# Moving the V-tile loads of a decode attention kernel from SyncE's DMA queue to ScalarE's

## The chip, the cores and the metric

One core of a Trainium2 chip runs the whole program once. The metric is device time in microseconds of that launch: 406.5 us, the median of three runs (406.42 to 406.69). The core has a matrix engine (TensorE, PE in the profile), a vector engine (VectorE, DVE), an activation engine (ScalarE, ACT), GpSimd (POOL) and SyncE (SP). Each runs its own list of instructions in order and waits on semaphores that the others and the DMA transfers raise. Sixteen DMA engines move data between the chip's main memory and the on-chip buffers.

## The reference, cut to what matters

One token (S = 1, D = 1024) passes an attention block with a cache of 65536 keys in 4 groups, each shared by 8 of 32 query heads of width 128, and, beside it, a small MLP mixer; both are added to the input.

```python
xn = _layernorm(x)
q  = xn @ wq                                   # 32 heads x 128
scores = einsum(q, k) * 128 ** -0.5            # k, v: 4 groups x 65536 keys x 128, bf16
p  = softmax(scores)
A  = einsum(p, v).reshape(4096) @ wo
h  = gelu(layernorm(xn) @ w1)                  # its parts are shifted by one or two tokens
x1 = xn + shifted(h) @ w2
B  = x1 + gelu(layernorm(x1) @ w3) @ w4
return x + A + B
```

With one token, the shifted parts of `h` are all zero; the kernel keeps those products. The two caches are 67 MB each, and with the weights nearly 170 MB are read once.

## The kernel before, in words

Everything large arrives in one of five equal buffers, the slots (`SLOTS = 5`, pool `big`, L61), each 128 partitions x 32 KB, 4 MiB in all. `items` (L82 to L91) lists the loads in order: two halves of wq; then for each of 4 groups g and 4 blocks r of 16384 keys the pair K(g,r), V(g,r); two halves of w3 after block (0,1), w1 after (1,1), a quarter of wo after each group; at the end w2 and w4 in five pieces of 16, 8, 2, 1 and 1 rows per partition. In this text K12 is group 1, block 2. wo, w1 and w2 loads are 2 MiB, the w3 halves 3.5 MiB.

The loop at L440 asks for the loads up to four items ahead (`ensure`, L129), then records the work on the current one. A load can only be issued when its slot is open, that is, when the last reader of the slot's former tenant is done. All loads of `items` are issued by SyncE (L118), so they stand in one queue in this order.

Work on a K tile (`compute_K`, L342): four in-place 32x32 transposes on VectorE (L353), each followed by eight scoring products of 512 keys on TensorE (L357). After the last of these the slot is open. Then comes a short chain: `mx` on VectorE (L361), a TensorE transpose (L363), `m8` and `rep` on VectorE (L365, L367), a TensorE transpose back (L370), `nball` (L372), the exponential on ScalarE (`p_sb`, L374), and its transpose on VectorE (`pT`, L377).

Work on a V tile (`compute_V`, L382): 32 products with `pT` on TensorE (L389), after which the slot is open, and a copy `ob` on ScalarE (L394). After the fourth block `group_end` (L399) merges the four blocks: `negmg`, `wts`, `og` (L402 to L409), `pm_e` (L417, L419), `msk`, `rl`, `o5`, `oT5` (L421 to L428). `compute_wo` (L431) multiplies `oT5` with the wo quarter into the output rows (`psB`, L160); w2 and w4 are added to the same rows at the end.

The order on each engine is not that of the source. The framework's scheduler takes the recorded instructions and orders each engine's list by when it expects operands to be there, and it also decides which open slot the next tile gets. In the built kernel of before, VectorE does the whole chain of one K tile up to `pT` before it starts transposes of the next one. Two small loads of the input go over ScalarE's queue at the start (L123, L125), and four small transfers of the MLP over GpSimd's queue (L288, L290).

Of the kernel before, what the change touches and what calls it, by code (L numbers as in the profile page):

```python
# [22 lines left out]
def kernel(  # L23
# [14 lines left out]
    nc = tc.nc  # L38
# [56 lines left out]
    def slot():  # L95
        return big.tile([P, KEYS], BF16, name="slot")

    def issue(item):
        kind = item[0]
        t = slot()  # L100
        if kind == "wq":
            src = wq_v[:, 4 * item[1]:4 * item[1] + 4, :].rearrange("p c n -> p (c n)")
        elif kind == "w3":
            src = w3_v[:, 4 * item[1]:4 * item[1] + 4, :].rearrange("p c n -> p (c n)")
        elif kind == "w4":
            c0 = w4_start[item[1]]
            src = w4_v[:, c0:c0 + W4_PIECES[item[1]], :].rearrange("p c n -> p (c n)")
        elif kind == "w1":
            src = w1_v
        elif kind == "w2":  # L110
            src = w2_v
        elif kind == "wo":
            src = wo_v[item[1]]
        else:
            cache = A_k_cache if kind == "K" else A_v_cache
            _, g, r = item
            src = cache[0, g, r * KEYS:(r + 1) * KEYS, :].rearrange("(p k) d -> p (k d)", p=P)
        nc.sync.dma_start(out=t[:, 0:src.shape[-1]], in_=src)  # L118
        st[item] = t


# [7 lines left out]
    def ensure(upto):  # L129
        while n_issued[0] <= min(upto, len(items) - 1):  # L130
            issue(items[n_issued[0]])
            n_issued[0] += 1
# [85 lines left out]
    for cg in range(4):  # L218
        nc.vector.tensor_copy(out=selbig[:, cg, :].rearrange("p (hl dd) -> p hl dd", dd=16),
                              in_=sel32[:, 8 * cg:8 * cg + 8].unsqueeze(2).to_broadcast([P, 8, 16]))  # L220
    sel8big = const.tile([P, P], F32, name="sel8big")
    nc.vector.tensor_copy(out=sel8big[:].rearrange("p (hl dd) -> p hl dd", dd=16),
                          in_=sel8[:].unsqueeze(2).to_broadcast([P, 8, 16]))
# [3 lines left out]
    for b in range(2):  # L227
        for par in range(2):
            nc.vector.tensor_copy(out=psel[:, 2 * b + par, :].rearrange("p (a i) -> p a i", a=4),  # L229
                                  in_=iv[:, b, par, :].unsqueeze(1).to_broadcast([P, 4, 32]))  # L230
# [242 lines left out]
```

## Time and profile before

| what | us |
|---|---|
| median of three runs | 406.5 (406.42 to 406.69) |
| the profiled execution's own time | 406.69 |
| its span | 404.8 |
| PE / DVE / ACT busy | 245.7 / 215.7 / 37.7 |
| share of the span that the 16 DMA engines spend on SyncE's queue (q1) | 98.0% |
| mean rate of the DMA engines | 420 GB/s |
| issue to landing of a K load, of a V load (median) | 34.5, 35.5 |

The page of the profile gives the busy time of each engine, then the span in 40 slices (a digit is a busy share in tenths), the DMA queues, the chain of work that ended last, and groups of equal instructions with their busy time, the mean of one in ns, and the idle time in front of them with what ended most of it. In the waits, a row reads: engine and line, what it waited for, us in total, times, longest. In the timeline a row reads: start, us, engine, line, operation; SPq and ACTq rows are the issuing of a DMA, and the idle time before them is found in the waits of the queue. The instruction's source line is given as L353.

### The profile page before, as it was taken

How to read it: one execution, taken by the hardware profiler on the slowest of the kernel's cores; microseconds unless marked ns; L12 is line 12 of the kernel's file. 1: busy time of each engine (PE TensorE's matmuls, PEld its weight loads, DVE VectorE, ACT ScalarE, POOL GpSimd, SP SyncE). 2: the span in 40 equal slices, each digit the busy share in tenths (PEclk: the TensorE clock that was granted, in tenths of full speed). 3: DMA queues.
4: the chain of work that ended last, by engine and by line, in shares of the span. 5: the costliest groups of instructions: out<-in, count | busy, mean ns of one | idle time of the engine just before them, and what ended most of it. 6: DMA issues, size and time to landing. Idle time of an engine off the chain costs nothing.

```text
span 404.8 us, 3326 instructions
## 1 busy us (share of the span) xinstructions
PE 245.7 (61%) x1400; PEld 95.7 (24%) x1400; DVE 215.7 (53%) x235; ACT 37.7 (9%) x60; POOL 11.2 (3%) x30
## 2 busy tenths in 40 slices
PE   0385565328475847557657948384659474758456
PEld 0132222103132312112223313131233121213122
DVE  0419474017484848346665847475748383838500
ACT  0101101100201010120210010101010101010100
POOL 5001000000000000000010000000000000000000
PEclk9998878857795778768595868888958797679898
DMA  8999999999999999999999999999999999999993
GB/s 363 415 424 449 418 426 434 430 418 444 434 408 439 447 416 419 458 418 416 447 431 413 437 444 414 435 440 418 430 440 424 428 439 427 425 437 413 440 415 134
DMA packets 7065, 170.11 MB, mean 420 GB/s; under 512 B 1023, under 2 KB 1033, under 8 KB 1418
## 3 DMA queue, kind: packets, MB, share of 16 engines
q1 hardware_dynamic: 6772, 169.87, 98.0%
q8 instruction: 11, 0.18, 0.2%
q0 software_dynamic: 128, 0.02, 0.0%
q10 hardware_dynamic: 150, 0.01, 0.0%
q14 instruction: 4, 0.03, 0.0%
HBM read 169.88 MB, written 0.01 MB: 420 GB/s over the span
## 4 chain that ended last, share of the span: by engine, by line
DMA 54%; PE 23%; DVE 17%; ACT 2%; another core or an unknown queue 1%; issue 1%; DVEq 0%; ACTq 0%
DMA slot<-in_A_k_cache_dram 44%; DVE slot L353 11%; PE sc L357 10%; DMA slot<-in_B_w_dram 7%; PE psB L160 5%; PE oacc L389 4%; DMA x_bf<-in_A_x_dram 3%; DVE pT L377 2%; DVE mx L361 2%; ACT p_sb L374 2%; PE rows L244 1%; PE pm_e L417 1%; DVE m L365 0%; PE pm_mx L363 0%
## 5 line engine op out<-in xcount | busy, mean ns | idle before, releaser
L353 DVE STREAM_TRANSPOSE slot<-slot 128x2048 f32<-128x2048 f32 x64 | 142.3, 2281 | 61.1 <-DMA slot<-in_A_k_cache_dram 61.1
L357 PE MATMUL sc<-slot,qst 128*128 128x512 bf16 x512 | 131.6, 411 | 40.9 <-DVE slot L353 40.9
L389 PE MATMUL oacc<-slot,pT 128*32 128x512 bf16 x512 | 56.0, 616 | 48.0 <-DVE pT L377 48.0
L357 PEld LDWEIGHTS <-qst 128*128 128x128 bf16 x512 | 51.6, 103 | 125.1 <-issue 45.9
L361 DVE TENSOR_REDUCE mx<-sc 128x1 f32<-128x1024 f32 x16 | 19.6, 1225 | 34.7 <-PE sc L357 34.7
L374 ACT ACTIVATE p_sb<-sc,nball 128x1024 bf16<-128x1024 f32 x16 | 17.8, 1114 | 209.8 <-DVE nball L372 209.8
L389 PEld LDWEIGHTS <-pT 128*32 128x32 bf16 x512 | 17.5, 139 | 75.0 <-DVE pT L377 49.4
L377 DVE STREAM_TRANSPOSE pT<-p_sb 128x1024 bf16<-128x1024 bf16 x16 | 19.9, 1245 | 23.3 <-ACT p_sb L374 23.3
L244 PE MATMUL rows<-slot,xpad 128*32 128x512 bf16 (+1 forms) x144 | 13.6, 509 | 6.1 <-DMA slot<-in_B_w_dram 6.1
L363 PE MATMUL pm_mx<-ident_f,mx 128*1 128x128 f32 x16 | 4.3, 270 | 21.1 <-DVE mx L361 21.1
L160 PE MATMUL psB<-slot,oT 128*1 128x512 bf16 x64 | 12.6, 564 | 4.3 <-DVE oT L428 4.3
L394 ACT COPY ob<-oacc 128x512 f32<-128x512 f32 x12 | 7.0, 586 | 58.6 <-PE oacc L389 58.6
L160 PE MATMUL psB<-slot,dst_h 128*1 128x512 bf16 x56 | 7.9, 444 | 3.2 <-DMA slot<-in_B_w_dram 3.2
L370 PE MATMUL pm_mx<-ident_f,rep 1*128 1x1 f32 x16 | 3.5, 222 | 9.9 <-DVE rep L367 9.9
L417 PE MATMUL pm_e<-og,selbig 128*128 128x128 f32 x32 | 7.4, 403 | 3.4 <-DVE og L409 3.4
L244 PEld LDWEIGHTS <-xpad 128*32 128x32 bf16 x144 | 5.7, 127 | 15.0 <-issue 13.7
L172 PE MATMUL pm_ln<-ln_rowsum_a,ones_f 128*128 128x1 f32 x2 | 0.6, 348 | 13.6 <-DVE psel L229 13.6
L337 DVE CAST out<-psB 64x256 bf16<-64x256 f32 x1 | 0.4, 417 | 15.2 <-ACT out L336 15.2
L363 PEld LDWEIGHTS pm_mx<-ident_f,mx 128*1 128x1 f32 x16 | 1.3, 79 | 29.0 <-DVE mx L361 29.0
L417 PEld LDWEIGHTS pm_e<-og,selbig 128*128 128x128 f32 x32 | 6.3, 293 | 6.7 <-DVE og L409 6.7
L365 DVE TENSOR_REDUCE m<-pm_mx 1x8 f32<-1x128 f32 x16 | 4.4, 278 | 5.8 <-PE pm_mx L363 5.8
L374 ACT ACT_TABLE_LOAD x3 | 3.8, 1283 | 35.6 <-DVE nball L372 35.6
(97 smaller groups left out, 79.3 us busy)
## 6 DMA issues: line engine op xcount, KB each, us to landing
slot<-in_A_k_cache_dram SPq DMA_DIRECT2D x16, 4096.0 KB, 34.5
slot<-in_A_v_cache_dram SPq DMA_DIRECT2D x16, 4096.0 KB, 35.5
slot<-in_A_wq_dram SPq DMA_DIRECT2D x2, 4096.0 KB, 21.4
slot<-in_A_wo_dram SPq DMA_DIRECT2D x4, 2048.0 KB, 38.4
slot<-in_B_w_dram SPq DMA_DIRECT2D x2, 3584.0 KB, 42.6
slot<-in_B_w_dram SPq DMA_DIRECT2D x3, 2048.0 KB, 26.9
slot<-in_B_w_dram SPq DMA_DIRECT2D x1, 4096.0 KB, 27.8
slot<-in_B_w_dram SPq DMA_DIRECT2D x1, 512.0 KB, 16.1
```

The lines of the kernel that those rows point to most:

```text
L160: nc.tensor.matmul(psB[32 * j:32 * j + 1, :], lhsT=lhsT, rhs=rhs, start=(not row_started[j]), stop=False, tile_position=(0, 32 * j), skip_ ...
L244: nc.tensor.matmul(acc[32 * j:32 * j + 32, bk, 0:width], lhsT=xp[:, c, :], rhs=wt[:, cl, ch * width:(ch + 1) * width], start=(c == 0), sto ...
L353: nc.vector.transpose(out=kf[:, cg, :], in_=kf[:, cg, :])
L357: nc.tensor.matmul(sc[:, hf, :], lhsT=qst[g % 2][:, o:o + 128], rhs=kr[:, cg, hf, :, bp // 2, :, bp % 2], start=(cg == 0 and bp == 0), sto ...
L361: nc.vector.reduce_max(out=mx[:], in_=sc[:].rearrange("p h n -> p (h n)"), axis=AX.X)
L363: nc.tensor.transpose(pm[0:1, 0:P], mx[:, 0:1], ident_f[:])
L365: nc.vector.reduce_max(out=m8[:], in_=pm[0:1, 0:P].rearrange("o (j h) -> o h j", h=8), axis=AX.X)
L374: nc.scalar.activation(out=p_sb[:], in_=sc[:], func=ACTF.Exp, bias=nball[:, r:r + 1], scale=SCALE, accum_out=lall[:, r:r + 1])
L377: nc.vector.transpose(out=pT[:], in_=p_sb[:])
L389: nc.tensor.matmul(oacc[32 * u:32 * (u + 1), :], lhsT=pT[:, hf, 32 * t:32 * (t + 1)], rhs=vt[:, :, hf, t, :], start=(hf == 0 and t < 4), s ...
L394: nc.scalar.copy(out=ob[:], in_=oacc[:])
L417: nc.tensor.matmul(pe[:, 0:P], lhsT=selbig[:, cg, :], rhs=og[:, 128 * cg:128 * (cg + 1)], start=(cg == 0), stop=(cg == 3))
```

## The change

Where `issue` used to call SyncE for every tile, it now calls ScalarE for V tiles and SyncE for all others. The list of loads, the number of slots and the lookahead stay.

```diff
             src = cache[0, g, r * KEYS:(r + 1) * KEYS, :].rearrange("(p k) d -> p (k d)", p=P)
-        nc.sync.dma_start(out=t[:, 0:src.shape[-1]], in_=src)
+        eng = nc.scalar if kind == "V" else nc.sync
+        eng.dma_start(out=t[:, 0:src.shape[-1]], in_=src)
         st[item] = t
```

In the changed kernel every line after L117 has a number that is one higher, since the edit adds a line.

## The prediction

> **What bounds the kernel now.** I read the page's head and slices, then the queues, the chain, the waits, and the timeline of SyncE's issues.
>
> ```profile
> span 404.8 us, 3326 instructions
> DMA  8999999999999999999999999999999999999993
> q1 hardware_dynamic: 6772, 169.87, 98.0%
> DMA 54%; PE 23%; DVE 17%; ACT 2%; another core or an unknown queue 1%; issue 1%; DVEq 0%; ACTq 0%
> L353 DVE STREAM_TRANSPOSE slot<-slot 128x2048 f32<-128x2048 f32 x64 | 142.3, 2281 | 61.1 <-DMA slot<-in_A_k_cache_dram 61.1
> ```
>
> The 16 DMA engines are busy from the second slice to the last, 98.0% of it by q1, SyncE's queue; the vector engine idles 61.1 us for K tiles. The bound is the stream: 169.87 MB that may never pause. K03 (group 0, block 3) is first touched at 109.37 after 45.09 MB, K32 at 344.51 after 145.75 MB: 100.66 MB in 235.14 us, 428 GB/s. A 4 MiB tile takes 9.80 us, and a tile lands at bytes/428 GB/s + 4.0 us, 3.3 of which are latency (the first issue is at 0.74).
>
> What keeps the stream from pausing is the list of loads issued ahead:
>
> ```profile
> 120.33 0.33 SPq L118 DMA_DIRECT2D slot<-in_A_k_cache_dram  x1
> 129.20 0.33 SPq L118 DMA_DIRECT2D slot<-in_A_v_cache_dram  x1
> 136.98 0.33 SPq L118 DMA_DIRECT2D slot<-in_B_w_dram  x1
> 144.62 0.33 SPq L118 DMA_DIRECT2D slot<-in_A_k_cache_dram  x1
> 153.50 0.33 SPq L118 DMA_DIRECT2D slot<-in_A_v_cache_dram  x1
> ```
>
> These are K11, V11, w1, K12, V12. K11's last byte arrives near 152; V11, w1 and K12 were issued 8 to 23 us before that. An issue is made when a slot opens:
>
> ```profile
> SPq L118 <- PE oacc L389: 136.6, 16, 9.8
> SPq L118 <- DVE slot L353: 134.9, 16, 15.1
> ```
>
> The first row is waiting for the value product of a V tile, the second for work on a K tile (its scoring follows its transposes). So the change is worth what it does to slots opening.
>
> **The change part by part.**
>
> *The issues.* 16 V loads leave SP, where one costs 0.33 us (0.71 at most), for ACT: 16 x 0.33 = 5.3 us, at most 11, beside ACT's 209.8 us of idling for `nball`. No issue lies on the end's chain: zero. V00 now stands behind `ln_std_b` (ends 21.55) instead of at 2.13; 16 MB stand ahead on SP, and they cover it until 39 us. A V issue waiting for its slot holds what is behind it on ACT, mostly the next exponential or `ob` copy. The longest I find is V11's, until 153.5; the exponential behind it (K10) needs a score maximum that comes later. Zero again.
>
> *Two queues share the engines.* No load ran beside another here, so the split is bounded. q1's 6772 packets are 47 loads x (128 rows + 16) + 4: a row of 32 KB is a packet. Small transfers on the GpSimd queue landed in 6.5 to 7.3 us beside a full SP queue, less than the 9.80 of one tile, so another queue gets its turn between rows. I take turns row by row: equal shares of 32 KB rows, one third for a 16 KB-row weight. The ends are 2:1 in favour of K and 2:1 in favour of V.
>
> [...]
>
> *The scheduler rewrites the order.* This is the part that the diff hides. K loads are no longer behind V loads in one list, so the scheduler expects K early and puts transposes of the next K tile ahead of work of the last block. VectorE at the end of group 0:
>
> ```
> before: nball(K03) negmg | pT(K03) | og x4, lw | msk rl o5 oT5 | 4 transposes of K10
> after:  nball(K03) negmg | 4 transposes of K10 | pT(K03) | og x4, lw |
>         transpose of K11 | msk rl, mx(K10), o5 | transpose of K11 | oT5 ...
> ```
>
> Engines run in order. `pT(K03)`, which V03 needs, now waits for K10 to land, and `oT5`, which frees wo0's slot, for K11. The slots are handed out anew: V11 still follows V03, but w1 follows K10 and K12 follows wo0.
>
> *First dry spell.* K10 would land at 55.57 MB/428 + 4.0 = 133.8. V10 gets K03's slot when that is scored, 124.8, so from about 126.7 it shares while K10 has 5 to 6 us left, which doubles: K10 lands at 139.8. Four transposes (8.9; the timeline's x4 rows) to 148.7, `pT` 1.25, V03's product 3.6: V11 is issued at 153.5, where before had 129.20. K11, issued at 128.5, lands with all before it at 63.96 MB/428 + 4.0 = 153.4. At its last byte the five slots hold V03, wo0, K10, V10 and K11, and nothing is on order. Dry: 153.5 - 153.4 + 3.3 = 3.4 us.
>
> *Second dry spell.* At the end of group 1 the slots hold V12, K13, V13, wo1 and K20. K20 lands at 225.6. The next load, V20, takes K13's slot. K13 landed at 210.2, two transposes 214.6, K12's `mx` 215.9, its `m`, a third transpose and `rep` 218.9, TensorE's return of `rep` 219.2; 25 of K13's 32 scoring products stand behind that (25 x 0.236, from the 1.89 us of eight): 225.2. Dry: 225.2 - 225.6 + 3.3, about 3.0 (3.1 with waits added). At the end of group 2, V30 and K31 are issued at 308.7 and 308.2 and K30 lands at 311.9: just covered, 0 now, up to 2 if scoring is slower.
>
> The times between come from the same steps carried tile by tile. On the order of before they put K13's issue at 164.4 (trace 164.06) and K33's landing at 364.2 (363.99).
>
> *The tail.*
>
> ```profile
> 365.42 27.79 DMA slot<-in_B_w_dram
> 393.26 7.49 PE psB L160 x54
> ```
>
> Before, TensorE is through with wo3 and w2 at 390.07 and idles 3.19 us for w4. K33 now lands at 370.4, the dry spells later. Its chain to the end of wo3 was 24.3 us (363.99 to 388.3); V32's `pT` (1.25) and product (3.6) now stand inside it, 5.1 with their waits: less the 3.19 of slack and about 0.8 of waiting for the next w4 piece, which goes too, +1.1.
>
> Sum: 3.4 + 3.1 + 1.1 = +7.6 us. The profiled execution took 406.69 (span 404.8 and 1.9 around it), 0.2 over the median of 406.5: 414.3, and against the median 414.1.
>
> Bounds of the same sum: shares of 1.3:1 for SP +3.4, for ACT +12.2; 2:1 for SP +14, for ACT +20; scoring at 0.298 us (the row of 9.53 us x32) instead of 0.236, +11.7.
>
> **The rivals.**
>
> *Unequal sharing.* One queue gets markedly more, so K tiles, or in the tail V33 and w4, come far later: +12 to +20, 418 to 426. For it: no row shows two loads side by side. Against: equal packets.
>
> *The stream stays covered.* If tiles pass whole, K10 is finished before V10 begins, stays at 134, and V11 is issued some 6 us earlier, before K11's last byte: both spells go and the tail alone is left, +0.2 to +1.3, 406.7 to 407.8. For it: the next K still arrives in time for the new order; against: the 6.5 to 7.3 us of the small transfers. [...]
>
> *Faster.* Two queues raise the rate of the stream. Slices 2 to 39 average 429 GB/s, the better half of them 440, single ones 458. At 440 the bytes take 386 instead of 397 us: -11 + 7.6, about 403. It decides from a rate 1.9% up (7.6/397). Against: packets fill 98.0%, so there are no gaps to close, packets themselves would have to shorten.
>
> That the change does nothing is excluded: all 16 V loads stand on ACT in the built order.
>
> **How the numbers follow.** The forecast, two or three dry spells, +3 to +12 us: 0.62. Unequal sharing 0.12. Covered 0.17, of which nearly half is within 0.2%, about what a measurement can tell from no change (0.8 us). Faster 0.09. So faster 0.09, same 0.08, slower 0.83. Range: the forecast's own is 409.5 to 418.5; with the rivals 407 to 423 leaves out the faster case, a little of the covered one and the worst of unequal sharing.
>
> **What would show it.** V loads on ACT's queue with some 67 MB; slices near 150 and 225 us with lower GB/s and idle DMA; the landing of K tiles later than before by growing steps, to 6 us at K33; `pT` released by VectorE's own transposes; issue to landing of V loads falling from 35.5 to about 20 us, since they are issued later and share. It would be wrong if the stream has no gap (then the turn is coarser than a row), if the rate moves, or if the dry spells sit at other joints.

## The result, and the profile after

The changed kernel takes 409.21 us (median of 18 runs, 406.67 to 411.83) where the kernel before takes 406.53 (18 runs, 406.42 to 406.72). The ratio is 1.0072, with a 95% interval of 1.0055 to 1.009: slower by 0.7%, or 2.7 us. The forecast was slower by 7.6 us. All ratios in this document compare fast executions with fast ones; a single execution, of 412.97 us in the table of experiments, does not count as fast. Two things are to be explained: why the loss is only a third of the forecast, and why the executions of the changed kernel lie up to 5 us apart while those of the kernel before lie within 0.3 us.

These lines of the page of the changed kernel (the profiled execution took 407.21 us, near the low end of that range) answer to those shown of the kernel before:

```profile
span 405.4 us, 3336 instructions
DMA  8999999999999999999999999999999999999993
q1 hardware_dynamic: 4468, 102.76, 59.3%
q10 hardware_dynamic: 2454, 67.12, 38.7%
...
DMA 56%; PE 24%; DVE 15%; another core or an unknown queue 3%; issue 1%; ACT 0%; SPq 0%; DVEq 0%
...
L354 DVE STREAM_TRANSPOSE slot<-slot 128x2048 f32<-128x2048 f32 x64 | 144.9, 2289 | 108.3 <-DMA slot<-in_A_k_cache_dram 108.3
```

The change did what it says: ScalarE's queue (q10) carries 67.12 MB, the 16 V tiles. The two queues together fill 98.0% of the engines' time, as one did before, and no slice shows a hole. The chain of waits still goes by K tiles (56%, before 54%). VectorE idles 108.3 us for K tiles, before 61.1, although the time hardly moved: the waits were gathered in front of K's transposes, because those now stand ahead of work that used to be done while a K tile was on its way.

The loss lies in two places that a page does not show: in the stream, by which K33 lands late, and in the chain of work behind K33. They come out of one comparison over the profiles of this study. `wo3`'s first product into `psB` is the first thing that TensorE can do once the last group is merged. Before, it starts at 386.45 and TensorE later idles 3.19 us for w4. The table sets beside it when K33's transposes begin (K33 has landed) and the wait for w4's pieces:

| execution | K33's transposes | wo3's first product | from the one to the other | last wait for w4 ends | span |
|---|---|---|---|---|---|
| before | 363.99 | 386.45 | 22.5 | 393.26 | 404.8 |
| after (the page above) | 364.30 | 390.19 | 25.9 | none | 405.4 |
| copy 1 (again_a) | 364.23 | 389.15 | 24.9 | 398.00 | 404.6 |
| copy 2 (again_b) | 365.14 | 393.02 | 27.9 | none | 408.0 |
| copy 3 (after_again_c) | 367.97 | 396.83 | 28.9 | none | 411.9 |

Where TensorE waits for nothing any more, the span ends 15.0 to 15.2 us after `wo3`'s first product. Where it waits for w4's last pieces (copy 1), the span ends 6.6 us after them. So the kernel before has 3.19 us of room between its last chain and the stream, and the changed kernel has used that up: K33 +0.31, chain +3.43, less 3.19 is +0.55 for the execution above (span +0.6); +1.15 +5.42 -3.19 = +3.4 for copy 2 (+3.2); +3.98 +6.40 -3.19 = +7.2 for copy 3 (+7.1).

The chain of waits shows which of the two ends an execution. First the end of the changed kernel (start us, us, what):

```profile
364.30 2.32 DVE slot L354
...
383.06 2.94 PE oacc L390 x32
390.19 11.57 PE psB L161 x88
```

then that of copy 1, the same kernel:

```profile
379.74 18.22 DMA slot<-in_B_w_dram
398.00 2.54 PE psB L161 x22
```

In copy 1 the weights still come last, as before. In the execution of the page, and in copies 2 and 3, TensorE has no wait for w4 left in which anything could hide.

### The profile page after: what moved, and what is told of

Same layout as the page of the kernel before. It is cut to its first block, busy times and chain, and to the rows that moved or that the text cites. A ratio compares the mean times of both kernels' runs of the same rounds, so it can differ in the third digit from the quotient of the medians.

```text
span 405.4 us, 3336 instructions
## 1 busy us (share of the span) xinstructions
PE 232.6 (57%) x1400; PEld 90.2 (22%) x1400; DVE 210.5 (52%) x235; ACT 37.6 (9%) x60; POOL 11.2 (3%) x30
## 3 DMA queue, kind: packets, MB, share of 16 engines
q10 hardware_dynamic: 2454, 67.12, 38.7%
## 4 chain that ended last, share of the span: by engine, by line
DMA 56%; PE 24%; DVE 15%; another core or an unknown queue 3%; issue 1%; ACT 0%; SPq 0%; DVEq 0%
DMA slot<-in_A_k_cache_dram 56%; PE sc L358 14%; DVE slot L354 11%; PE psB L161 4%; PE oacc L390 3%; DVE mx L362 2%; PE pm_e L418 1%; DVE pT L378 1%; PE rows L245 1%; PE pm_mx L371 0%; PE pm_mx L364 0%; ACT p_sb L375 0%; DVE o L425 0%; SPq L119 0%
## 5 line engine op out<-in xcount | busy, mean ns | idle before, releaser
L358 PE MATMUL sc<-slot,qst 128*128 128x512 bf16 x512 | 148.7, 448 | 107.1 <-DVE slot L354 93.5
L354 DVE STREAM_TRANSPOSE slot<-slot 128x2048 f32<-128x2048 f32 x64 | 144.9, 2289 | 108.3 <-DMA slot<-in_A_k_cache_dram 108.3
L358 PEld LDWEIGHTS <-qst 128*128 128x128 bf16 x512 | 53.2, 109 | 188.7 <-issue 77.5
L390 PE MATMUL oacc<-slot,pT 128*32 128x512 bf16 x512 | 38.8, 451 | 14.2 <-DVE pT L378 14.2
L375 ACT ACTIVATE p_sb<-sc,nball 128x1024 bf16<-128x1024 f32 x16 | 17.8, 1115 | 180.5 <-DVE nball L373 180.4
L390 PEld LDWEIGHTS <-pT 128*32 128x32 bf16 x512 | 14.0, 108 | 36.1 <-DVE pT L378 17.8
L395 ACT COPY ob<-oacc 128x512 f32<-128x512 f32 x12 | 7.0, 587 | 80.7 <-PE oacc L390 80.7
L161 PE MATMUL psB<-slot,oT 128*1 128x512 bf16 x64 | 9.9, 464 | 1.1 <-DVE oT L429 1.1
L364 PEld LDWEIGHTS pm_mx<-ident_f,mx 128*1 128x1 f32 x16 | 1.4, 88 | 24.9 <-DVE mx L362 22.3
L245 PEld LDWEIGHTS <-xpad 128*32 128x32 bf16 x144 | 4.7, 117 | 7.8 <-issue 6.2
L161 PE MATMUL psB<-slot,dst_h 128*1 128x512 bf16 x56 | 6.2, 379 | 0.0
L371 PEld LDWEIGHTS pm_mx<-ident_f,rep 1*128 1x128 f32 x16 | 2.4, 150 | 16.5 <-DVE rep L368 11.8
## 6 DMA issues: line engine op xcount, KB each, us to landing
slot<-in_A_v_cache_dram ACTq DMA_DIRECT2D x16, 4096.0 KB, 24.2
```

The costliest lines, as they stand in the source:

```text
L161: nc.tensor.matmul(psB[32 * j:32 * j + 1, :], lhsT=lhsT, rhs=rhs, start=(not row_started[j]), stop=False, tile_position=(0, 32 * j), skip_ ...
L245: nc.tensor.matmul(acc[32 * j:32 * j + 32, bk, 0:width], lhsT=xp[:, c, :], rhs=wt[:, cl, ch * width:(ch + 1) * width], start=(c == 0), sto ...
L354: nc.vector.transpose(out=kf[:, cg, :], in_=kf[:, cg, :])
L358: nc.tensor.matmul(sc[:, hf, :], lhsT=qst[g % 2][:, o:o + 128], rhs=kr[:, cg, hf, :, bp // 2, :, bp % 2], start=(cg == 0 and bp == 0), sto ...
L364: nc.tensor.transpose(pm[0:1, 0:P], mx[:, 0:1], ident_f[:])
L371: nc.tensor.transpose(pm[:, P:P + 1], rep[0:1, :], ident_f[0:1, 0:1])
```

## The experiments

| kernel | median, us | all runs | ratio to before (95%) |
|---|---|---|---|
| the changed kernel again, one run each | 406.4, 409.83 | | |
| the changed kernel again, five rounds | 410.71 | 409.11 to 413.72 | 1.0093 (1.0072 to 1.0114) |
| two queues, vector order of before | 414.06 | 413.3 to 414.82 | 1.0183 (1.0167 to 1.0199) |
| one queue, every `pT` behind the next K's transposes | 407.48 | 406.98 to 408.4 | 1.0027 (1.0018 to 1.0036) |
| one queue, the last such pair alone | 407.53 | 406.51 to 408.56 | 1.0026 (1.0017 to 1.0036) |
| changed kernel, last pair in the order of before | 408.48 | 406.8 to 409.98 | 1.0042 (1.0025 to 1.006) |
| changed kernel, all joints (the steps from one group to the next) and the last pair | 410.81 | 410.65 to 412.76 | 1.0112 (1.0094 to 1.013) |
| changed kernel, three holds in the last group | 407.88 | 406.6 to 412.97 | 1.0034 (1.0016 to 1.0052) |
| changed kernel, longer V products | 409.52 | 408.71 to 411.94 | 1.0082 (1.0054 to 1.011) |
| kernel before, longer V products | 406.61 | 406.38 to 406.76 | 1.0 (0.999 to 1.0009) |

The kernel before stood beside each at 406.5 to 406.7.

### The changed kernel three times more

No edit. The question is what differs between executions of one program.

> The changed kernel once more, for a second profiled execution, since its 18 runs lie between 406.67 and 411.83 while those of the kernel before lie within 0.3. Theory A (thin cover): whatever this execution takes over 407.2, shows as DMA engines idling near 150, 220 or 305 us, where all five slots are full, and in later landings of K tiles behind that point. Theory B (rate): a slower execution has no idle stretch, its DMA engines move fewer GB/s throughout and K tiles land later by growing steps.

> As the run before: a third profiled execution of the changed kernel. Theory A: an excess over 407.2 us equals the sum of idle stretches of the DMA engines at the joints of groups, to 1 us. Theory B: no idle stretch, a lower rate everywhere.

> The changed kernel unchanged, timed beside the others: 409 with a spread of 4 to 5 us, as in its 18 runs. Both theories expect it; its profile adds a fourth look at the tail. By theory C its excess over 406.5 equals its time from K33's landing to the end of the last output product, less 36 us.

Measured: 406.4, 409.83, and 410.71 in five rounds. The three profiles are in the table above. Copy 1 had no excess to explain. Copy 2 bears out neither theory: its stream is 0.26 MB (0.6 us) short of the kernel before at 390 us, as in the page's execution (0.25), and its excess is K33's 1.15 us and above all the chain behind it, 5.42 us longer than before. The rule set for copy 3 (K33 to the last product, less 36 us) gives 4.3 us of excess where 7.2 were measured; it leaves out the 4.0 by which K33 itself is late.

One difference is at the third joint, from group 2 to group 3, where V30's slot opens only after the scoring of K23 and the product of V22. That product in the timeline of TensorE, in the changed kernel and then in copy 3 (its file has one line more at the top, so L391 is L390):

```profile
298.89 1.91 PE L390 MATMUL oacc<-slot,pT 128*32 128x512 bf16 x32
...
301.22 1.91 PE L391 MATMUL oacc<-slot,pT 128*32 128x512 bf16 x32
```

V30 is issued at 300.91 in the one and at 303.24 in the other (1.7 of the 2.3 us are there already when K23's transposes begin, at 281.61 and 283.33; 0.6 are the scoring just before the product, 5.09 and 5.70 us), and the stretches of 2 us behind it (columns: busy us of the engines, TensorE's granted clock, DMA share, GB/s) read, for the changed kernel

```profile
302.00:304.00 2.00, 0.49 (x2) 0.21 (x2) 1.19 (x5) 0.16 (x1) 0.00 (x0) 1.00 0.90 377
304.00:306.00 2.00, 0.00 (x0) 0.00 (x0) 1.26 (x1) 1.23 (x3) 0.00 (x0) 0.83 1.13 475
```

and for copy 3

```profile
302.00:304.00 2.00, 1.45 (x25) 0.41 (x13) 0.51 (x1) 0.58 (x1) 0.00 (x0) 1.00 0.57 246
304.00:306.00 2.00, 0.49 (x2) 0.21 (x2) 1.29 (x4) 0.00 (x0) 0.00 (x0) 1.00 0.94 262
```

852 against 508 GB/s over two stretches of 2 us: 0.69 MB less in copy 3. Part of it comes back by 310 us; from 300 to 310 us copy 3 loses 0.49 MB on the kernel before, 1.1 us of stream. That is a short dry spell, at the joint which the forecast called "just covered, 0 now, up to 2 if scoring is slower". More of the spread is made in the tail, where the same lists run at a mean granted clock (364 to 390 us) of 0.82 in the changed kernel's page, 0.87 in copy 1, 0.74 in copy 2 and 0.76 in copy 3; the last section shows how the clock steps.

### Two queues, with the vector order of before

```diff
+            if st.get("last_dve") is not None:
+                with tc.issue_after(st["last_dve"]):      # last pT or oT5
+                    nc.vector.transpose(out=kf[:, cg, :], in_=kf[:, cg, :])
+            else: ...
```

All four transposes of every K tile stand behind the `pT` or `oT5` before them. In the trace VectorE's order is that of the kernel before, but for two transposes early in the run and one memset, so the queues are nearly all that differs.

> V loads on ScalarE's queue as in the change, but VectorE's transposes of a K tile are made to stand behind the pT (or oT) of the block before, as in the kernel before. Theory A (row turns, and slots that open late because of the order): no idle stretch of the DMA engines, since V slots open early again; but K33 shares with V33 and lands near 374, 10 us later than in the kernel before, and its chain of 24 us to the end of wo3, then w2 and w4, ends 6 us later: 412 to 413. Rival C (only the rewritten order costs): the order is undone, so 406.5.

Measured: 414.06 us, a little over the 412 to 413 of theory A and far from the rival's 406.5. The order alone is therefore not what costs: with the old order two queues are worse by 3 to 5 us than with the new one. The stream is whole (0.08 MB ahead of the kernel before at 390 us). But V loads are issued early, as before, and now take half of the engines from the K tile that stands ahead of them in the list: from 355 to 365 us 2.16 MB go over SyncE's queue and 2.10 over ScalarE's. The timeline of VectorE:

```profile
373.33 8.89 DVE L356 STREAM_TRANSPOSE slot<-slot 128x2048 f32<-128x2048 f32 x4 [3.33 <-DMA slot<-in_A_k_cache_dram]
```

K33 lands at 373.33, 9.34 later than before. From there to `wo3`'s first product it takes 23.1 us, as before; 9.34 + 0.6 - 3.19 = +6.8, and the span is 411.4 (+6.6). No byte came late in sum; the wrong bytes came first.

### One queue, with the order of after

Two kernels with one queue. In the first every `pT` stands behind the next K tile's transposes, in the second V32's alone.

```diff
+            tr = nc.vector.transpose(out=kf[:, cg, :], in_=kf[:, cg, :])
+            if (g, r) == (HKV - 1, NT - 1) and cg == 3:      # in the first: (g, r) != (0, 0) and cg == 3
+                ...
+                tc.add_manual_dep(st["last_pT"], tr.name, ..., reason="order")
```

> The kernel before on one queue, with pT of every K tile made to stand behind the four transposes of the next K tile, so each V slot opens only when the next K has landed: the order of the change, everywhere and more strictly, without its queues. Theory C: slots open later but the stream stays covered, since the next K comes before the V behind it on one queue; the same tail as in the run before it: 407 to 409. Theory A (order alone dries the stream): idle stretches at the joints, 412 or more.

> The kernel before, all loads on SyncE's queue, with only the order of the tail taken from the change: pT of K32 is made to stand behind K33's four transposes. Theory C: K33 lands at 364.0, V32's pT and product (1.25 + 1.9 to 3.6) move into its chain, the slack of 3.2 us is used up: 407 to 409, and the spread grows from 0.3 to 2 us or more although the queues are untouched. Rival (the split of the queues is what costs): 406.5, spread 0.3.

Measured: 407.48 and 407.53 us, +0.9 and +1.0. Both keep the stream whole (within 0.1 MB at 390 us) and K33 in its place (363.76 and 363.77). As far as the profiles show, all of the loss is in the tail, and the last pair alone makes it; the chain of the second:

```profile
382.19 3.63 PE oacc L395 x18
...
390.02 11.35 PE psB L160 x81
```

26.25 us from K33 to `wo3`'s first product, +3.8 on before; less 3.19 of room and -0.2 for K33, +0.4 (span +0.2). Both profiled executions (406.98 and 406.82) are faster than their medians, so the whole +0.9 and +1.0 stand in no profile. The spread is there too: 1.4 and 2.1 us with untouched queues, where the kernel before, timed beside them, has 0.45. The other joints in the new order cost nothing on one queue. With the two queues this makes a square: one queue 406.5 (old order) and 407.5 (about the new), two queues 414.1 and 409 to 411.

### The changed kernel, with the tail's order of before

```diff
+            if (g, r) == (HKV - 1, NT - 1):
+                with tc.issue_after(st["last_pT"]):
+                    nc.vector.transpose(out=kf[:, cg, :], in_=kf[:, cg, :])
+            else: ...
```

> The changed kernel, in which only the last K tile's four transposes are made to stand behind pT of the block before (K32), as in the kernel before. Theory C (the stream is as fast as before, the excess is the tail: V32's pT and its product stand inside the chain from K33 to the end, so TensorE's speed in the last 35 us decides each execution): K33 still lands at 364 to 365, the chain to the end of wo3 falls back to 23 to 24 us, and 18 of 18 executions end with the stream: 406.4 to 407.2, spread under 1 us. Theory A (dry spells at the joints of groups): nothing at the end matters to it, 408.5 to 410 with the same spread.

Measured: 408.48 us, at the lower end of theory A's time and not within theory C's; its spread is 3.2 us, where theory C expected under 1. The chain from K33 is down to 23.9 us and waits for w4 again; what is left is the stream. Its end, in the chain of waits:

```profile
376.92 22.85 DMA slot<-in_B_w_dram
399.81 2.54 PE psB L161 x22
```

w4's last pieces are awaited until 399.81, 1.8 later than in copy 1, and the bytes moved by 310 us are 0.81 MB (1.9 us) short of the kernel before, 0.36 MB of it lost between 300 and 310 us. So the tail is one part of the loss, and the stream, most visibly at the third joint, the other.

### Both parts taken away

First with holds at every joint of the groups and in the tail, then, since that cut the scoring of K32 in two, with three holds in the last group alone.

```diff
-            if (g, r) == (HKV - 1, NT - 1):
+            if (g, r) == (HKV - 1, NT - 1) or (g > 0 and r == 0):              # first
+            if (g, r) in ((HKV - 1, NT - 1), (HKV - 1, 0), (HKV - 1, 2)):      # second; K32 behind pT(K30)
```

The first edit keeps the `issue_after` of the experiment before; in the second, K32's transposes stand behind the `pT` before the last one.

> The changed kernel, with the transposes of the first K tile of each later group, and of K33, held behind the pT of the block before (the kernel before's order at the joints of the groups and in the tail; inside the groups the changed kernel's order stays). Theory D, the excess of 2.7 us is made at the joints and in the tail: 406.4 to 407.5 us, executions within 1.5 us of each other, K33 landing by 365, the last chain TensorE idling for w4 or the stream as in the kernel before. Rival, the two queues lose rate wherever V loads come late, whatever the order at the joints: 408.5 to 410 us, bytes moved by 390 us 0.5 MB or more behind the kernel before. A third outcome, 411 to 415: holding the joints lets V loads share with K tiles as in the run where the whole old order was kept on two queues (414), and K33 lands past 370.

> The changed kernel with three holds in the last group alone: K30's transposes behind pT(K23), K32's behind pT(K30), K33's behind pT(K32); all before that as in the changed kernel. It is meant to take away the late V30 at the third joint and the longer tail together, without cutting K32's scoring in two as the holds at every joint did (there K33's transposes began at 369.3). Theory D, joint and tail are all of the excess: 406.4 to 407.6 us, bytes moved by 390 us within 0.2 MB of the kernel before, K33's transposes starting by 367. Rival E, on two queues every earlier V load makes a K tile later and the last chain pays for it: stream whole, K33's transposes or K32's mx 3 us or more later than in the run with the tail hold alone (366.05 and 358.05), and 409 to 411 us.

Measured: 410.81 and 407.88 us. Neither gave both at once. The first repaired the stream (0.06 MB short at 390 us; V30 issued at 296.00), and the tail paid for it. K33's transposes did not wait for K33 but for what stood ahead of them on VectorE:

```profile
364.24 1.23 DVE L366 TENSOR_REDUCE mx<-sc 128x1 f32<-128x1024 f32 x1 [6.55 <-PE sc L362]
...
369.33 8.85 DVE L356 STREAM_TRANSPOSE slot<-slot 128x2048 f32<-128x2048 f32 x4
```

The scheduler had put the `pT` of K30 and K31 next to each other between K32's transposes, so two value products cut K32's scoring in two, and `mx` of K32 came at 364.24 where the run with the tail hold had 358.05. This meets the time of the third outcome (411 to 415) nearly, by another way than the one it named. The second lies between the times of theory D and rival E. It kept the tail short (K33 at 365.92, 23.9 us to `wo3`) and left the stream 0.72 MB short at 310 us: V30, issued at 302.37, waits for V22's product behind K23's scoring, which a hold on K30 does not move. The theory that joint and tail are all of the excess is neither shown nor refuted by these two; no kernel on two queues was found that keeps both, and none that beats the kernel before.

### Longer value products

Sixteen products more ahead of the 32 of each V tile (overwritten by them), in the changed kernel and, as a control, in the kernel before.

```diff
+        for t in range(16):
+            u = t % 4
+            nc.tensor.matmul(oacc[32 * u:32 * (u + 1), :], lhsT=pT[:, 0, 32 * t:32 * (t + 1)],
+                             rhs=vt[:, :, 0, t, :], start=(t < 4), stop=(t >= 16 - 4), ...)
```

> The changed kernel with half of each V tile's products done twice: 16 more products ahead of the 32, 0.9 us more per V tile by the 1.84 to 1.91 us that 32 take in the changed kernel. Theory A (thin cover, which the price of V's product decides): each V slot opens 0.9 us later and idle stretches of 1.5 to 2 us appear at 152 and 222 in most executions: 3 to 5 us over the changed kernel, 412 to 414. Theory B (rate): V's product is hidden, within 0.7 us of the changed kernel, 408.5 to 410.

> Control for the run with 16 extra products ahead of each V tile's 32: the same extra products in the kernel before, one queue, vector order unchanged. If a longer value product matters only where a V load is the next to go dry, it is hidden here, since loads are issued 8 to 23 us ahead of need: 406.3 to 406.9 us, V's slot-opening later by 1 to 2 us, no dry stretch. Rival, the extra products cost by themselves (TensorE time in the last group and the tail): 408 to 410 us, which would take the verdict of that earlier run away.

Measured: 409.52 us on two queues, 406.61 on one. In the groups of the changed kernel with the extra products, L395 and L389 are the 32 and the 16:

```profile
L395 PE MATMUL oacc<-slot,pT 128*32 128x512 bf16 x512 | 35.3, 424 | 0.0
...
L389 PE MATMUL oacc<-slot,pT 128*32 128x512 bf16 x256 | 19.4, 427 | 16.0 <-DVE pT L378 14.4
```

54.7 us over 16 tiles are 3.4 us a tile, about the 3.6 that the forecast had assumed. With them the stream does fall short at the joints where the forecast had it, though by less: against the kernel before it is 0.24 MB (0.6 us) short at 160 us, 0.73 (1.7 us) at 230 and 1.27 at 330, where the changed kernel is 0.04, 0.05 and 0.24 short. 1.24 MB at 390 us are 2.9 us, and the span of the profiled execution is 2.8 longer than before: w4's last pieces are awaited until 400.93. In time, though, the run cannot be told from the changed kernel: 409.52 lies between its 409.21 and 410.71, where theory B had it, and the 412 to 414 of theory A are missed. The order on VectorE and TensorE also differs in places from the changed kernel's. So the bytes support the forecast's mechanism, and the time does not. The control is clean: its products take 4.9 us a tile instead of 3.5 and the time does not move, since on one queue the loads are issued long before they are needed.

## Why the prediction was wrong in size

*The issues* (zero): right. A V load's issue takes 0.33 us on ScalarE, which idles 180.4 us for `nball`.

*Two queues share the engines* (equal turns, row by row): right. Three stretches of 1.2 us of the changed kernel, 29.1 to 32.7 us, when K and V loads run together (packets, MB, share):

```profile
q1 hardware_dynamic: 16, 0.52, 102.4%
...
q10 hardware_dynamic: 16, 0.52, 101.3%
...
q1 hardware_dynamic: 16, 0.52, 101.5%
```

16 rows of 32 KB for one queue, then 16 for the other; by the shares (101 to 102%) each 16 fill the 16 engines for their 1.2 us, one row for each. From 140 to 147 us the two queues move 1.51 and 1.57 MB. With that *Unequal sharing* falls, and *Faster* with the mean rate of 420 GB/s, the same as before. So the sign given for a coarser turn, a stream without gaps, misled: the turn is one row, and the first two joints still have no gap.

*The scheduler rewrites the order*: right. The timeline of the changed kernel at the end of group 0 shows it, and where the next step failed:

```profile
134.77 8.89 DVE L354 STREAM_TRANSPOSE slot<-slot 128x2048 f32<-128x2048 f32 x4 [1.93 <-DMA slot<-in_A_k_cache_dram]
143.59 1.20 DVE L378 STREAM_TRANSPOSE pT<-p_sb 128x1024 bf16<-128x1024 bf16 x1
...
145.22 1.91 PE L390 MATMUL oacc<-slot,pT 128*32 128x512 bf16 x32
...
147.18 0.33 ACTq L119 DMA_DIRECT2D slot<-in_A_v_cache_dram  x1
148.35 0.33 SPq L119 DMA_DIRECT2D slot<-in_B_w_dram  x1
...
154.30 2.31 DVE L354 STREAM_TRANSPOSE slot<-slot 128x2048 f32<-128x2048 f32 x1 [6.37 <-DMA slot<-in_A_k_cache_dram]
```

*First dry spell* (+3.4): this step failed. V11 was to be issued at 153.5, just after K11's last byte; it is issued at 147.18, and K11 is touched at 154.30, 7.1 us later. That covers the 3.3 us of latency that the forecast had worked out, and the bytes moved by 160 us are 0.04 MB short: nothing was lost here. Of the 6.3 us by which V11 is early, 5.0 are K10's landing, by 134.77 and not 139.8. The other 1.3 lie behind it: V03's product was taken at 3.6 us and took 1.91, and 0.4 us of waits go against that. In the kernel before, TensorE had waited 2.83 us ahead of V03's product; in the changed kernel it follows 27 scoring products without a pause.

K10 lands early because it is not shared. The forecast let V10 begin at 126.7, with 5 to 6 us of K10 to come. V10 is issued at 129.61, and the queues (packets, MB, share) read, for 130 to 131 us and for 132 to 133 us,

```profile
q1 hardware_dynamic: 15, 0.49, 114.2%
...
q10 hardware_dynamic: 13, 0.43, 98.7%
```

K10 is all but through when V10 begins. V10 takes the slot of K03, and K03, which shares with V02 and V03 (issued at 77.68 and 83.81), is first touched at 117.89. Forecast was an open slot at 124.8; with the 11.7 us that lie between the two in the trace, that is K03 at about 113 (an estimate). How much of this comes from the price of the V products is not shown: V00's took 1.91, but V01's 3.43, near the assumed 3.6, and the forecast gave no times for V02 and V03. The run with longer products shows that the chain hangs together in this way: V02 and V03 issued later (78.56, 85.71), K03 touched earlier (116.41), V10 issued earlier (128.12), K10 later (135.85), V11 later (149.51).

*Second dry spell* (+3.1): this failed too, and in K13's landing, not in V's product. The timeline:

```profile
202.00 4.50 DVE L354 STREAM_TRANSPOSE slot<-slot 128x2048 f32<-128x2048 f32 x2 [9.49 <-DMA slot<-in_A_k_cache_dram]
...
217.74 0.34 ACTq L119 DMA_DIRECT2D slot<-in_A_v_cache_dram  x1
...
221.65 8.89 DVE L354 STREAM_TRANSPOSE slot<-slot 128x2048 f32<-128x2048 f32 x4 [0.68 <-DMA slot<-in_A_k_cache_dram]
```

K13 is touched at 202.00 (forecast 210.2), V20 issued at 217.74 (225.2), K20 touched at 221.65 (225.6). From K13 to V20 it takes 15.7 us, the forecast had 15.0. So V20 is 7.5 us early and K20 only 4.0: 217.74 - 221.65 + 3.3 is -0.6, barely covered, and 0.05 MB are missing by 230 us. 3.4 us of each are the first spell that did not come; why K13 is 4.8 earlier still is open.

*End of group 2* ("just covered, 0 now, up to 2 if scoring is slower"): right, and this margin is a part of the spread, though the lateness comes more from K23's landing than from its scoring. The stream is 0.25 to 1.14 MB (0.6 to 2.7 us) short at 390 us in the four profiles of the changed kernel; copy 3 lost 0.49 MB of it between 300 and 310 us, as shown above. Some 0.4 to 0.5 MB are missing by 300 us in every one of them, most of it lost after 230 us, and at which loads was not found.

*The tail* (+1.1): the mechanism is right and was underrated. V32's `pT` and product stand inside K33's chain, and the 3.19 us of room are gone. K33 lands at 364.3 to 368.0, not 370.4, as the dry spells did not come; but the chain is 2.5 to 6.4 us longer where the forecast had 5.1. In the typical copy 2 it is 5.4, V32's product taking 3.42 and V33's 3.58, so the tail alone is worth 5.4 - 3.19 = +2.2. The 0.8 us that the forecast took off for w4's next piece do not show in the sum: w4's products take 6.21 us instead of 7.88, but wo3 and w2 take 5.1 to 5.3 instead of 3.62.

The rival *The stream stays covered* (406.7 to 407.8) was right about the first two joints, down to K10 finishing before V10 begins and V11 coming some 6 us earlier. The reason was another: tiles do not pass whole, V10 came 4.8 us later than forecast. Of the forecast's signs, the 67.12 MB on ScalarE's queue came, and V loads land 24.2 us after their issue; the gaps near 150 and 225 us and a K33 6 us late (0.3 in the page's execution, 4.0 in copy 3) did not. That the time fell near the forecast's own 409.5 to 418.5 is no support for it: both spells are absent, and a longer tail and smaller losses of the stream stand in for them.

What the forecast did not have at all is that the new order also protects: by holding V loads back it keeps K33 from landing at 373, and without it two queues would have cost 7.5 us. That this is the size of the forecast's sum is chance; the loss there came another way.

## What to carry to other kernels

Moving loads to a second queue added no rate here, where one queue already filled the engines (98.0%, and 420 GB/s with one and with two); it lets a later load take half of them (1.57 of 3.08 MB from 140 to 147 us) from the one that is needed first, so ask which tile of a pair is on the path before splitting the pair. Read the room at the end of the chain (here 3.19 us of waiting for w4) as a budget: a change that spends it shows little in the median at first and much in the spread. Before a duration is taken from a row into a new place, see what the engine did just before it in that row, and at which granted clock it ran.

## What the runs showed of the hardware that was not expected

The same 32 value products take 3.60 us at a granted clock of 0.50 and 1.91 at 1.00. What stands before them goes along with it: in the kernel before, all 16 products had an idle TensorE in front of them while it waited for `pT` (48.0 us in sum), and each took 3.17 to 3.61 us. After the change 6 had (14.2 us) and took 3.43, 3.61, 3.60, 3.58, 1.91 and 2.92 us, while nine of the other ten took 1.91 each; the median of one matmul of these products went from 634 to 379 ns. The stretches with the granted clock, of V03's product before

```profile
125.50:129.20 3.70, 3.60 (x32) 1.08 (x32) 1.90 (x5) 0.00 (x0) 0.00 (x0) 0.50 1.01 434
```

and of the scoring and V03's product after

```profile
137.20:145.20 8.00, 8.00 (x27) 2.96 (x27) 8.00 (x8) 0.00 (x0) 0.00 (x0) 0.73 1.04 451
145.20:147.10 1.90, 1.90 (x34) 0.80 (x34) 1.49 (x4) 0.00 (x0) 0.00 (x0) 1.00 0.72 310
```

show 0.50 against 1.00. But it does not decide alone. V32's product has the same work in front of it in all four profiles of the changed kernel, 31 scoring products and then 0.88 us of idling; it takes 1.91 us in the page's execution and in copy 1, and 3.42 and 3.40 in copies 2 and 3. The clock around it, in the page's execution (product at 378.08) and in copy 2 (at 379.73):

```profile
370.15:383.81 13.66, 8.54 (x75) 3.62 (x77) 8.34 (x13) 2.00 (x6) 0.00 (x0) 1.00 1.01 428
...
379.42:382.83 3.41, 3.10 (x32) 1.08 (x32) 0.62 (x3) 0.00 (x0) 0.00 (x0) 0.50 1.11 476
```

These are whole stretches of one clock, four times 3.41 us and once. In six traces (the kernel before, the page's execution, copies 1 and 2, two queues with the vector order of before, and the longer products on two queues) the granted clock is, from 29 us on, 1.00 or 0.50 and changes only at steps of 3.41 us, on a grid that lies elsewhere in each: its first point after 30 us is at 31.10, 32.24, 31.66, 31.26, 31.50 and 30.67 us. The copies run the same lists of instructions on every engine. So the same list meets the steps differently each time, and the tail of the changed kernel, run at a mean clock of 0.74 to 0.87, takes 24.9 to 28.9 us from K33 to `wo3`.

What sets the clock at a step no run here shows. The kernel before can hide a longer product in its 3.19 us of room: with the extra products V33's part takes 5.1 us instead of 3.17, `wo3` begins at 388.46 and not 386.45, and the time stays.
